# A gated linear recurrence and its MLP on one core: the score and state products laid into halves of the PE array's columns

## The chip, the cores and the metric

The kernel runs on one core of a Trainium2 chip, in one launch. The metric is the device time of that core in microseconds. The engines' short names are those of the profile: PE (TensorE, products), PEld (its weight loads, which may lie beside products), DVE (VectorE), ACT (ScalarE), POOL (GpSimd), and SP, whose queue issues the transfers.

## What is computed

A GateLoop recurrence for 4 sequences of 768 tokens, 8 heads of 48 elements each, followed by one MLP with the activation h * erf(softplus(h)):

```python
mag = np.sqrt(a_re * a_re + a_im * a_im)
scale = np.minimum(mag, 0.999) / (mag + 1e-06)
a_re_n, a_im_n = (a_re * scale, a_im * scale)
for t in range(S):
    new_re = ar * S_re - ai * S_im
    new_im = ar * S_im + ai * S_re
    S_re, S_im = (new_re + kv, new_im)          # kv: outer product of k and v of token t
    y[:, :, t] = np.einsum('bhd,bhde->bhe', q[:, :, t], S_re)
...
h = x @ w_in                                    # x: 3072 x 384, w_in: 384 x 2048
sp = np.maximum(h, 0.0) + np.log1p(np.exp(-np.abs(h)))
return (h * erf(sp)) @ w_out                    # w_out: 2048 x 384
```

All data is float32.

## The kernel before, in words

The path that runs is `quotient_path` (a second, slower path stands behind a test of the data at the end, and isn't taken here). It takes the recurrence in **chunks** of 128 tokens. Within a chunk the running product of the gates is a quotient of two prefix products, so that the tokens of a chunk meet in a masked product of queries and keys, as in linear attention, and chunks are joined by a state S. Two chunks make a **unit** of 256 tokens; there are 12 units, so 24 chunks, and six chunks make one sequence. The first chunk of a sequence has no state to read, the last one none to write.

Per unit, in the order of the work:

- `load_gates`, `load_qkv` (line 687): transfers on SP's queue. Values v go into one of two buffers `v0`, `v1`, by pairs of heads: 48 elements of the even head, a gap of 16 zeros, 48 of the odd head. `side` gives the part of one head. A transfer for each chunk and each of the two sides, four a unit.
- `g_mag` to `g_decay`: the gates' logarithms, angles and their prefix sums (the products `sum`, lines 818, 820 and 837), sines, and exponentials.
- `chunk(u, c)`: ten steps. `prep` (line 865) scales and turns k and q (tiles kt, qt: 128 tokens x 8 heads x 96). `cols` (line 876) turns four heads at a time so that the 96 elements lie on the partitions (products `tr`, line 880, then a copy: by ACT for k, by DVE for q). `state` (line 898) makes the chunk's sum of k v products, 96 x 48 for each head (`kv`, line 903), adds the old state and scales with w, the gates' product over the chunk (lines 912, 914). `scores` (line 887), once for each four heads: a product of 128 keys by 128 queries for each head (`sc`, line 891), then one DVE product with the upper triangle `triu` (line 894), which gives A. `xT` (line 917) makes the output of the chunk, already turned: the 384 output columns are cut in pieces of 32, each put into one quarter of the array's columns (`y`, line 940): v times A, and, but for the first chunk, the old state times q.
- `ff_in` (line 950): h = x w_in, 16 tiles of 128 columns in two slabs (`hps`, line 960), copied out by ACT. `softplus` (line 966): four activations over a slab of 2048 elements per partition. `erf_times_h` (line 978), in four parts of 512: Gelu on ACT into e (line 988), and four DVE operations (lines 989 to 992), the first of which writes the tile t. `ff_out` (line 996): the second product (`ops`, line 1006), then a copy and a transfer out.

Each engine works its instructions in order. The order is set in two steps: a list `plan` gives each step a due time in units (lines 1048 on), sorted before the program is recorded, and then a scheduler of the language may move an instruction past others on its engine where no data forbids it. Buffers are limited on purpose: z and yy of the softplus have one buffer, e two, A two (one for each four heads), kt one. PSUM has four pools of two buffers: `ps_a` for tr and sc, `ps_b` for sum, kv and y, `ps_h` for hps, `ps_o` for ops. Transfers wait on SP's queue in its order too.

In the profile a product in float32 appears as two passes, each a weight load (PEld) and a matmul (PE). In a form such as `128*32 128x128`, the first pair is rows and columns of the loaded weights, the second the streamed operand.

Of the kernel before, what the change touches and what calls it, by code (L numbers as in the profile page):

```python
# [10 lines left out]
FP = mybir.dt.float32  # L11
# [5 lines left out]
OP = mybir.AluOpType  # L17
PSUM = bass.MemoryType.PSUM

P = 128  # L20
# [27 lines left out]
def product_path(  # L48
# [280 lines left out]
    def attention(u, c, hg):  # L329
# [43 lines left out]
        def diag():  # L373
            lv = ps_lv.tile([P, HG, P], FP, tag="lv", name="dg")
            for j in range(HG):
                nc.tensor.matmul(out=lv[:, j, :], lhsT=st["K"][0:D2, j, :], rhs=st["q0"][0:D2, j, :],
                                 start=True, stop=True)
            A = att2.tile([P, HG, P], FP, tag="A", name="A")
            nc.vector.tensor_tensor(out=A, in0=lv, in1=ident.unsqueeze(1).to_broadcast([P, HG, P]), op=OP.mult)
            st["A"] = A  # L380

        def level(l):
            def f():
                m = 1 << l
                nb = P // (2 * m)
                Q, K, A, tot = st["Q"], st["K"], st["A"], st["tot"]
                Qv = Q.rearrange("p h (b w m) -> p h b w m", w=2, m=m)
# [5 lines left out]
                def halves(t, w):  # L393
                    return t.rearrange("p h (b w m) -> p (h b) w m", w=2, m=m)[:, :, w, :]
                nc.vector.copy_predicated(out=halves(A, 1), mask=pair[l], data=lv.rearrange("p h b m -> p (h b) m"))

# [160 lines left out]
def quotient_path(  # L557
# [19 lines left out]
    nc = tc.nc  # L577
    B, H, S, D = q.shape
    D2 = 2 * D
# [4 lines left out]
    C = 2  # L584
    NT = C * P
    PER = S // NT
    NU = B * PER
    HG = 4
# [6 lines left out]
    const = ctx.enter_context(tc.tile_pool(name="const", bufs=1))  # L595
# [4 lines left out]
    att1 = ctx.enter_context(tc.tile_pool(name="att1", bufs=1))  # L600
    att2 = ctx.enter_context(tc.tile_pool(name="att2", bufs=2))
# [3 lines left out]
    yp = ctx.enter_context(tc.tile_pool(name="yp", bufs=1))  # L605
    op = ctx.enter_context(tc.tile_pool(name="op", bufs=2))
# [7 lines left out]
    T = {}  # L614
# [1 line left out]

    ident = const.tile([P, P], FP, name="ident")
    make_identity(nc, ident)
    triu = const.tile([P, P], FP, name="triu")
    make_upper_triangular(nc, triu, val=1.0, diag=True)  # L620
    ones = const.tile([P, 1], FP, name="ones")
    nc.vector.memset(ones, 1.0)
# [13 lines left out]

    GAP, QUAD = 16, P // 4
    PAIR = 2 * D + GAP  # L640
    vbuf = [const.tile([P, C, H // 2, PAIR], FP, name=f"v{i}") for i in range(2)]
    sbuf = [const.tile([P, H // 2, PAIR], FP, name=f"S{i}") for i in range(2)]
    for t in vbuf:
        nc.vector.memset(t[:, :, :, D:D + GAP], 0.0)
# [3 lines left out]
    def side(t, e):  # L648

        return t[..., e * (D + GAP):e * (D + GAP) + D]  # L650
# [19 lines left out]
    def rows(a, u, c):  # L670
        b, s = divmod(u, PER)
        t0 = (s * C + c) * P
        return a[b, :, t0:t0 + P, :].rearrange("h t d -> t h d")
# [13 lines left out]
    def load_qkv(u):  # L687
        if 0 <= u < NU:
            load(ldq, "q", q, u)
            load(ldq, "k", k, u)  # L690
            t = T["v", u] = vbuf[u % 2]
            for c in range(C):
                for e in range(2):
                    src = rows(v, u, c).rearrange("t (h e) d -> e t h d", e=2)[e]
                    nc.sync.dma_start(out=side(t[:, c], e), in_=src)


    def narrow(i, dst, src, shape, home):
# [160 lines left out]
    def chunk(u, c):  # L859
# [3 lines left out]
        st = {}  # L863

        def prep(nm, e):
            def f():
                a = att1.tile([P, H, D], FP, tag="part", name=nm + "r", bufs=2)
                nc.vector.tensor_tensor(out=a, in0=T[nm, u][:, c], op=OP.mult,
                                        in1=T["pr", u][:, c, e, :].rearrange("p (h d) -> p h d", d=D))
                t = att1.tile([P, H, 2, D], FP, tag=nm + "t", name=nm + "t")  # L870
                cs = T["CS", u][:, c].rearrange("p u (h d) -> p h u d", d=D)
                nc.vector.tensor_tensor(out=t, in0=a.unsqueeze(2).to_broadcast([P, H, 2, D]), in1=cs, op=OP.mult)  # L872
                st[nm] = t
            return f
# [12 lines left out]
        def scores(g):  # L887
            def f():
                ps = ps_a.tile([P, HG, P], FP, tag="a", name="sc")
                for j in range(HG):  # L890
                    nc.tensor.matmul(out=ps[:, j, :], lhsT=st["k", g][0:D2, j, :], rhs=st["q", g][0:D2, j, :],  # L891
                                     start=True, stop=True)
                A = att2.tile([P, HG, P], FP, tag="A", name="A")
                nc.vector.tensor_tensor(out=A, in0=ps, in1=triu.unsqueeze(1).to_broadcast([P, HG, P]), op=OP.mult)
                st["A", g] = A
            return f

        def state():
            if last:
                return  # L900
            kv = ps_b.tile([P, H, D], FP, tag="b", name="kv")
            for j in range(H):
                nc.tensor.matmul(out=kv[0:D2, j, :], lhsT=st["k"][:, j].rearrange("p u d -> p (u d)"),  # L903
                                 rhs=side(T["v", u][:, c, j // 2], j % 2), start=True, stop=True)
            ns = sbuf[(u * C + c) % 2]
            w = T["w", u, c][0:D2].unsqueeze(2).to_broadcast([D2, H, D])
            if first:
                t = kv
            else:
                t = att1.tile([P, H, D], FP, tag="part", name="Skv", bufs=2)  # L910
                for e in range(2):
                    nc.vector.tensor_tensor(out=t[0:D2, e::2, :], in0=kv[0:D2, e::2, :], in1=side(T["S"][0:D2], e), op=OP.add)
            for e in range(2):
                nc.vector.tensor_tensor(out=side(ns[0:D2], e), in0=t[0:D2, e::2, :], in1=w[:, e::2, :], op=OP.mult)
            st["S"] = ns
# [62 lines left out]
    def erf_times_h(u, sl):  # L978

        n = SLAB // 4  # L980

        def part(i):
            def f():
                ss = slice(i * n, (i + 1) * n)
                h, z, y = (T[nm, u, sl][:, ss, :] for nm in ("h", "z", "yy"))
                t = yp.tile([P, n, NT], FP, tag="t", name="t")
                e = yp.tile([P, n, NT], FP, tag="e", name="e", bufs=2)
                act(out=e, in_=z, func=AF.Gelu, scale=RT2)
                nc.vector.tensor_tensor(out=t, in0=z, in1=y, op=OP.mult)  # L989
                nc.vector.scalar_tensor_tensor(out=y, in0=t, scalar=-2.0, in1=y, op0=OP.add, op1=OP.mult)  # L990
                nc.vector.tensor_tensor(out=e, in0=e, in1=y, op=OP.mult)  # L991
                nc.vector.scalar_tensor_tensor(out=h, in0=e, scalar=1.0 / RT2, in1=h, op0=OP.add, op1=OP.mult)  # L992
            return f
        return [part(i) for i in range(SLAB // n)]
# [50 lines left out]
    for cc in one:  # L1045
        g_sin(0, cc)

    plan = list(zip((0.50, 0.51, 0.52, 0.53, 0.55, 0.56, 0.60, 0.58, 0.59, 0.66), chunk(0, 0)))
    plan += list(zip((0.54, 0.57, 0.61, 0.62, 0.63, 0.64, 0.70, 0.68, 0.69, 0.74), chunk(0, 1)))
    plan += [(0.565, wt[0][2]), (0.645, wt[1][1]), (0.646, wt[1][2]), (0.71, wt[2][1]), (0.71, wt[2][2])]  # L1050
    plan += [(0.60, partial(load_qkv, 1))] + [(0.605, wt[j][0]) for j in (4, 5)]
# [9 lines left out]
    for j in range(6, len(wt)):  # L1061
        b = 1.45 + 1.1 * (j - 6) / (len(wt) - 6)
# [4 lines left out]
    for u in range(NU):  # L1067
        if u > 0:
            for c in range(C):
                b = begins[u][c] if u in begins else u + 0.5 * c  # L1070
# [10 lines left out]
        for sl in range(NSL):  # L1081
            b = u + 1.05 + 0.45 * sl
            plan += at(*(inputs[u][sl] if u in inputs else (b, b + 0.35)), ff_in(u, sl))
            b = u + 2.6 + 0.35 * sl
# [7 lines left out]
    n = len(seen)  # L1092
# [3 lines left out]
    ps = ps_b.tile([P, n], FP, tag="b", name="all")  # L1096
# [58 lines left out]
```

## Time and profile before

| | |
|---|---|
| three runs | 769.97, 774.02, 771.62 us; median 771.62 |
| the profiled execution | 771.92 us; the span of its instructions 770.1 us |
| mean granted clock of TensorE | 0.981 |
| instructions in the profile | 11542 |
| HBM read, written | 36.24 MB, 4.75 MB |
| transfers of v | 48 issues of 96 KB |

Where a page or a view says span, it counts from the first profiled instruction to the last; the 1.8 us between it and the execution's time lie around them. "Busy" is the time in which at least one instruction of a group is under way, so the mean length of a matmul, which holds its latency, times the count can be far over the busy time. A digit of a row by slices is the busy share of 19.25 us in tenths. In a group's line the last part is the time that the engine was idle just ahead of the group's instructions, and what ended most of it. An idle engine that isn't the bound costs nothing.

### The profile page before, as it was taken

Reading aid. Unit: us, or ns where it says so; the run is one execution under the profiler, and the core shown is the slowest. Engines: PE = TensorE matmul, PEld = TensorE weight load, DVE = VectorE, ACT = ScalarE, POOL = GpSimd, SP = SyncE. Lnnn points to the kernel's source line nnn. Section 1 sums busy time; section 2 is a strip of 40 time slices with the busy share of each in tenths; the row PEclk is TensorE's granted clock in tenths of the full one; section 3 lists DMA queues with packets and bytes.
Section 4 is the critical chain, followed back from the end, with each engine's and each line's share of the span. In section 5 each row is a group of like instructions: output and inputs, shape, how many; then the busy total and the mean of one; then the engine's idle time right before and its main releaser. Section 6 shows DMA issues by size and latency. Waiting matters only on the chain.

```text
span 770.1 us, 11542 instructions
## 1 busy us (share of the span) xinstructions
PE 720.1 (94%) x4524; PEld 542.0 (70%) x4524; DVE 535.7 (70%) x898; ACT 598.4 (78%) x815; POOL 1.1 (0%) x8
## 2 busy tenths in 40 slices
PE   1788869989999999999999999999999999999996
PEld 0566758866767777777777777777777777777553
DVE  5888978667887667567667668468567579765650
ACT  7889998698896993993993993993992888888810
POOL 0000000000000000000000000000000000000000
PEclk9998989999999999999999999999999999999998
DMA  8836456122212212212212212211112000000000
GB/s 218 219 109 163 103 114 179 29 41 43 41 43 52 42 32 53 43 31 52 42 32 52 42 31 47 48 31 38 16 32 42 1 21 1 1 22 0 21 20 26
DMA packets 148263, 41.84 MB, mean 54 GB/s; under 512 B 142292, under 2 KB 145384, under 8 KB 147432
## 3 DMA queue, kind: packets, MB, share of 16 engines
q1 hardware_dynamic: 148200, 41.02, 23.4%
q8 instruction: 37, 0.61, 0.3%
q14 instruction: 26, 0.21, 0.1%
HBM read 36.24 MB, written 4.75 MB: 53 GB/s over the span
## 4 chain that ended last, share of the span: by engine, by line
PE 62%; ACT 22%; DVE 9%; DMA 3%; issue 2%; SPq 1%; ACTq 0%; DVEq 0%
PE ops L1006 24%; PE hps L960 21%; ACT z L663 5%; ACT yy L663 4%; PE y L940 4%; PE sc L891 4%; PE tr L880 4%; ACT L662 3%; PE kv L903 3%; DVE t L989 2%; PE sum L818 2%; DVE yy L990 2%; PE sum L837 2%; DVE e L991 1%; ACT h L962 1%
## 5 line engine op out<-in xcount | busy, mean ns | idle before, releaser
L960 PE MATMUL hps<-xT,w_in_sb 128*128 128x256 f32 x1152 | 268.6, 383 | 4.4 <-ACT xT L944 2.6
L1006 PE MATMUL ops<-w_out_sb,h 128*128 128x384 f32 x768 | 267.2, 492 | 3.6 <-DVE h L992 2.8
L960 PEld LDWEIGHTS hps<-xT,w_in_sb 128*128 128x128 f32 x1152 | 217.0, 192 | 44.9 <-ACT xT L944 5.2
L1006 PEld LDWEIGHTS ops<-w_out_sb,h 128*128 128x128 f32 x768 | 141.8, 191 | 88.5 <-issue 5.3
L989 DVE TENSOR_TENSOR t<-z,yy 128x512 f32<-128x512 f32 x96 | 66.0, 688 | 57.5 <-ACT yy L663 56.9
L883 DVE COPY qT<-tr 96x512 f32<-96x512 f32 x48 | 32.8, 685 | 88.2 <-PE tr L880 88.1
L962 ACT COPY h<-hps 128x512 f32<-128x512 f32 x96 | 55.0, 575 | 50.0 <-PE hps L960 49.8
L662 ACT ACT_TABLE_LOAD x69 | 88.5, 1283 | 2.0 <-PEq L1139 0.8
L663 ACT ACTIVATE e<-z 128x512 f32<-128x512 f32 x96 | 57.4, 625 | 32.0 <-DVE h L992 31.8
L990 DVE SCALAR_TENSOR_TENSOR yy<-t,yy 128x512 f32<-128x512 f32 x96 | 66.0, 687 | 0.9
L991 DVE TENSOR_TENSOR e<-e,yy 128x512 f32<-128x512 f32 x96 | 64.8, 686 | 2.2 <-DVE yy L990 0.5
L992 DVE SCALAR_TENSOR_TENSOR h<-e,h 128x512 f32<-128x512 f32 x96 | 64.8, 686 | 0.2
L891 PE MATMUL sc<-qT,kT 96*128 96x128 f32 x384 | 50.4, 278 | 3.4 <-DVE qT L883 3.4
L891 PEld LDWEIGHTS sc<-qT,kT 96*128 96x128 f32 x384 | 47.7, 192 | 6.2 <-DVE qT L883 3.3
L940 PE MATMUL y<-A,v 128*32 128x128 f32 x768 | 47.6, 290 | 3.6 <-ACT pr L663 2.8
L663 ACT ACTIVATE z<-h 128x2048 f32<-128x2048 f32 x24 | 46.1, 1920 | 3.9 <-DVE t L989 3.8
L940 PEld LDWEIGHTS y<-A,v 128*32 128x32 f32 x768 | 34.7, 112 | 16.5 <-ACT pr L663 3.4
L663 ACT ACTIVATE yy<-z 128x2048 f32<-128x2048 f32 x24 | 45.9, 1913 | 0.4
L663 ACT ACTIVATE z<-z 128x2048 f32<-128x2048 f32 x24 | 45.9, 1912 | 0.4
L663 ACT ACTIVATE yy<-yy 128x2048 f32<-128x2048 f32 x24 | 45.9, 1912 | 0.2
L940 PE MATMUL y<-qT,S 96*32 96x128 f32 x640 | 41.0, 279 | 0.0
L880 PE MATMUL tr<-ident,kt 128*96 128x128 f32 x192 | 27.7, 280 | 8.0 <-DVE kt L872 7.6
(81 smaller groups left out, 792.2 us busy)
## 6 DMA issues: line engine op xcount, KB each, us to landing
raw<-in_moe_w_in_dram SPq DMA_DIRECT2D x6, 1024.0 KB, 7.2
raw<-in_moe_w_out_dram SPq DMA_DIRECT2D x8, 768.0 KB, 4.5
ar<-in_a_re_dram SPq DMA_DIRECT2D x24, 192.0 KB
ai<-in_a_im_dram SPq DMA_DIRECT2D x24, 192.0 KB, 3.5
q<-in_q_dram SPq DMA_DIRECT2D x24, 192.0 KB, 3.5
k<-in_k_dram SPq DMA_DIRECT2D x24, 192.0 KB, 3.2
v<-in_v_dram SPq DMA_DIRECT2D x48, 96.0 KB, 2.6
out_dram<-o SPq DMA_DIRECT2D x24, 192.0 KB, 1.9
```

The lines of the kernel that those rows point to most:

```text
L662: in_order(nc.scalar.preload_act_table_set(sets[0]))
L663: in_order(nc.scalar.activation(func=func, **kw))
L880: nc.tensor.transpose(out=ps[0:D2, j, :], in_=st[nm][:, g * HG + j].rearrange("p u d -> p (u d)"), identity=ident)
L891: nc.tensor.matmul(out=ps[:, j, :], lhsT=st["k", g][0:D2, j, :], rhs=st["q", g][0:D2, j, :], start=True, stop=True)
L940: nc.tensor.matmul(out=ps[b * QUAD:(b + 1) * QUAD, i, :], lhsT=lhsT, rhs=rhs, start=start, stop=stop)
L960: nc.tensor.matmul(out=ps[:, e, :], lhsT=w_in_sb[:, kd, f0:f0 + P], rhs=T["xT", u][:, kd, :], start=(kd == 0), stop=(kd == KD - 1))
L962: nc.scalar.copy(out=T["h", u, sl][:, i:i + 2, :], in_=ps)
L989: nc.vector.tensor_tensor(out=t, in0=z, in1=y, op=OP.mult)
L990: nc.vector.scalar_tensor_tensor(out=y, in0=t, scalar=-2.0, in1=y, op0=OP.add, op1=OP.mult)
L991: nc.vector.tensor_tensor(out=e, in0=e, in1=y, op=OP.mult)
L992: nc.vector.scalar_tensor_tensor(out=h, in0=e, scalar=1.0 / RT2, in1=h, op0=OP.add, op1=OP.mult)
L1006: nc.tensor.matmul(out=ps, lhsT=T["h", u, sl][:, e, jj * P:(jj + 1) * P], rhs=w_out_sb[:, i, :], start=(i == 0), stop=(i == KF - 1))
```

## The change

Five things are changed.

1. **Scores.** The score products of two heads are made as two pairs. The first pair takes keys 0 to 63 of each of the two heads against all 128 queries: the even head writes to PSUM partitions 0 to 63, the odd head to 64 to 127, so that they use different halves of the array's columns. The second pair takes keys 64 to 127 against queries 64 to 127 only, with the halves exchanged. The quarter of keys 64 to 127 and queries 0 to 63, which the mask makes zero, is left out; A is now two fixed buffers that are zeroed once. For odd heads the key halves stand exchanged on the partitions. The mask product is three DVE operations for four heads: one for the late 64 queries on all partitions, with a second mask `late` for the exchanged heads, and one each for the early queries of even and odd heads on 64 partitions.
2. **v.** As A of odd heads has its key halves exchanged, v of odd heads is loaded with its halves exchanged, in two transfers of 64 tokens, and once more in plain order into `odd0` or `odd1` for the state products. Eight transfers a unit, for four.
3. **State.** Each head's kv product is made as two of 64 columns, into PSUM partitions 0 to 63 and 64 to 127. The second takes columns 64 to 127 of a head's 96 in kt, so it runs 32 columns into its neighbour's; those results aren't read. kt is now a fixed buffer with 32 zeroed columns behind it.
4. **erf_times_h.** The tile t is gone: its product is written over z, which Gelu reads.
5. **The plan.** The state step of the very first chunk is due at 0.535 for 0.60, ahead of the preparation of the second chunk's k, which now writes the same fixed buffer.

```diff
-    triu = const.tile([P, P], FP, name="triu")
+    masks = const.tile([P, P + P // 2], FP, name="masks")
+    triu = masks[:, 0:P]
     make_upper_triangular(nc, triu, val=1.0, diag=True)
...
+    HALF = P // 2
+    abuf = [const.tile([P, 4, P], FP, name=f"A{i}") for i in range(2)]
+    for t in abuf:
+        nc.vector.memset(t, 0.0)
+    late = masks[:, HALF:].rearrange("p (e t) -> p e t", e=2)
+    nc.vector.tensor_copy(out=late[0:HALF, 1, :], in_=triu[0:HALF, 0:HALF])
+    nc.vector.memset(late[HALF:P, 1, :], 1.0)
+    kbuf = const.tile([P, H * 2 * D + P - 2 * D], FP, name="kt")
+    nc.vector.memset(kbuf[:, H * 2 * D:], 0.0)
...
+    vodd = [const.tile([P, C, H // 2, D], FP, name=f"odd{i}") for i in range(2)]
...
-                for e in range(2):
-                    src = rows(v, u, c).rearrange("t (h e) d -> e t h d", e=2)[e]
-                    nc.sync.dma_start(out=side(t[:, c], e), in_=src)
+                src = rows(v, u, c).rearrange("t (h e) d -> e t h d", e=2)
+                nc.sync.dma_start(out=side(t[:, c], 0), in_=src[0])
+                nc.sync.dma_start(out=vodd[u % 2][:, c], in_=src[1])
+                nc.sync.dma_start(out=side(t[HALF:P, c], 1), in_=src[1][0:HALF])
+                nc.sync.dma_start(out=side(t[0:HALF, c], 1), in_=src[1][HALF:P])
...
-                t = att1.tile([P, H, 2, D], FP, tag=nm + "t", name=nm + "t")
+                if nm == "k":
+                    t = kbuf[:, 0:H * 2 * D].rearrange("p (h u d) -> p h u d", h=H, u=2)
+                else:
+                    t = att1.tile([P, H, 2, D], FP, tag=nm + "t", name=nm + "t")
...
-                for j in range(HG):
-                    nc.tensor.matmul(out=ps[:, j, :], lhsT=st["k", g][0:D2, j, :], rhs=st["q", g][0:D2, j, :],
-                                     start=True, stop=True)
-                A = att2.tile([P, HG, P], FP, tag="A", name="A")
-                nc.vector.tensor_tensor(out=A, in0=ps, in1=triu.unsqueeze(1).to_broadcast([P, HG, P]), op=OP.mult)
-                st["A", g] = A
+                lo, hi = slice(0, HALF), slice(HALF, P)
+                for j in range(0, HG, 2):
+
+                    for keys, queries, out_ in ((lo, slice(0, P), (lo, hi)), (hi, hi, (hi, lo))):
+                        for e in range(2):
+                            nc.tensor.matmul(out=ps[out_[e], j + e, queries], lhsT=st["k", g][0:D2, j + e, keys],
+                                             rhs=st["q", g][0:D2, j + e, queries], start=True, stop=True)
+                A = st["A", g] = abuf[g]
+                pairs = lambda t: t.rearrange("p (h e) t -> p h e t", e=2)
+                nc.vector.tensor_tensor(out=pairs(A)[..., hi], in0=pairs(ps)[..., hi], op=OP.mult,
+                                        in1=late.unsqueeze(1).to_broadcast([P, HG // 2, 2, HALF]))
+                for e, r in enumerate((lo, hi)):
+                    nc.vector.tensor_tensor(out=A[r, e::2, lo], in0=ps[r, e::2, lo], op=OP.mult,
+                                            in1=triu[r, r].unsqueeze(1).to_broadcast([HALF, HG // 2, HALF]))
...
-                nc.tensor.matmul(out=kv[0:D2, j, :], lhsT=st["k"][:, j].rearrange("p u d -> p (u d)"),
-                                 rhs=side(T["v", u][:, c, j // 2], j % 2), start=True, stop=True)
+                val = vodd[u % 2][:, c, j // 2] if j % 2 else side(T["v", u][:, c, j // 2], 0)
+                for b in range(2):
+                    nc.tensor.matmul(out=kv[b * HALF:(b + 1) * HALF, j, :], rhs=val, start=True, stop=True,
+                                     lhsT=kbuf[:, j * D2 + b * HALF:j * D2 + (b + 1) * HALF])
...
-                t = yp.tile([P, n, NT], FP, tag="t", name="t")
                 e = yp.tile([P, n, NT], FP, tag="e", name="e", bufs=2)
                 act(out=e, in_=z, func=AF.Gelu, scale=RT2)
-                nc.vector.tensor_tensor(out=t, in0=z, in1=y, op=OP.mult)
-                nc.vector.scalar_tensor_tensor(out=y, in0=t, scalar=-2.0, in1=y, op0=OP.add, op1=OP.mult)
+                nc.vector.tensor_tensor(out=z, in0=z, in1=y, op=OP.mult)
+                nc.vector.scalar_tensor_tensor(out=y, in0=z, scalar=-2.0, in1=y, op0=OP.add, op1=OP.mult)
...
-    plan = list(zip((0.50, 0.51, 0.52, 0.53, 0.55, 0.56, 0.60, 0.58, 0.59, 0.66), chunk(0, 0)))
+    plan = list(zip((0.50, 0.51, 0.52, 0.53, 0.55, 0.56, 0.535, 0.58, 0.59, 0.66), chunk(0, 0)))
```

## The prediction, made before the changed kernel ran

> **What bounds the kernel now.** I read the page's first two parts, then the busy time by stretches of the span, then the groups of instructions, then a stretch of the timeline. The engines first; columns are busy time, share of the span, instructions, and below them the busy tenths of 40 slices of 19.25 us.
>
> ```profile
> PE 720.1 (94%) x4524; PEld 542.0 (70%) x4524; DVE 535.7 (70%) x898; ACT 598.4 (78%) x815; POOL 1.1 (0%) x8
> ...
> PE   1788869989999999999999999999999999999996
> ...
> DVE   5888978667887667567667668468567579765650
> ACT  7889998698896993993993993993992888888810
> ```
>
> TensorE is full from the seventh slice on; before that all engines are half full and none is. By stretches: 200 to 680 us has TensorE busy 118.3, 119.6, 119.6 and 120.0 of every 120 us, VectorE 83 to 84, ScalarE 94 to 98; 20 to 120 us has TensorE 80, VectorE 85, ScalarE 90 of 100. So some 20 of the 24 chunks lie where TensorE time is the kernel's time, and four lie in a start shared by VectorE, ScalarE and the transfers. What is to be changed there is small:
>
> ```profile
> L891 PE MATMUL sc<-qT,kT 96*128 96x128 f32 x384 | 50.4, 278 | 3.4 <-DVE qT L883 3.4
> L940 PE MATMUL y<-A,v 128*32 128x128 f32 x768 | 47.6, 290 | 3.6 <-ACT pr L663 2.8
> L903 PE MATMUL kv<-v,kt 128*96 128x48 f32 x320 | 31.9, 254 | 0.0
> ```
>
> Each product is two passes (192 score products give x384). The mean length of one holds pipeline latency; the price is the distance between starts, from the timeline (start, length):
>
> ```profile
> 400.98 1.48 PE L903 MATMUL kv<-v,kt 128*96 128x48 f32 x16
> 402.30 1.12 PE L891 MATMUL sc<-qT,kT 96*128 96x128 f32 x8
> 403.26 2.75 PE L1006 MATMUL ops<-w_out_sb,h 128*128 128x384 f32 x8
> ...
> 408.43 1.06 PE L891 MATMUL sc<-qT,kT 96*128 96x128 f32 x8
> 409.32 2.76 PE L960 MATMUL hps<-xT,w_in_sb 128*128 128x256 f32 x12
> 411.92 2.74 PE L1006 MATMUL ops<-w_out_sb,h 128*128 128x384 f32 x8
> 414.50 0.81 PE L818 MATMUL sum<-th,turns 128*128 128x384 f32 x2
> 415.24 0.43 PE L940 MATMUL y<-A,v 128*32 128x128 f32 x8
> ...
> 417.42 2.85 PE L1006 MATMUL ops<-w_out_sb,h 128*128 128x384 f32 x8
> 420.10 0.59 PE L960 MATMUL hps<-xT,w_in_sb 128*128 128x256 f32 x2
> ```
>
> Scores: 8 passes from 408.43 to 409.32, 0.112 us each. State: 16 passes in 1.32 us, 0.085 each apart from a short first. The 64 passes of y, in four column quarters, take 415.24 to 417.42, 0.034 each, though each streams as many columns as a score pass: quarters do run beside each other. But they have a price at the edges. Two passes of 384 columns cost 2.58/8 = 0.323 each, so sum should end at 415.15; y starts at 415.24 (0.09 late). The ops behind y take 2.68 to the next group, those ahead of it 2.58 (0.10 more: the first weights were not loaded beside earlier work). Between the last y pass (its four-row piece starts at 417.06, 0.42 long, passes 0.27: last start 417.21) and ops lie 0.21 instead of 0.11 (0.10).
>
> [...]
>
> **The change part by part.**
>
> Scores: a pair of heads was 4 passes at 0.112 = 0.448 us. Now each half of the columns gets two passes of 128 queries (0.112) and two of 64 [...], both halves at once: 0.340. A chunk of 4 pairs: 1.79 to 1.36.
>
> State: a chunk's 16 passes at 0.085, plus 0.07 [...] (kv and sc: 400.98 to 403.26 is 2.28 = 1.32 + 0.90 + 0.06), is 1.39. Now 16 passes in each half at 0.058: 0.93.
>
> Mode visits: every run of such products between products of the whole array pays 0.09 in, 0.05 for a first 64-column load that nothing hides (half of the 0.10 of 128), 0.10 out, 0.10 for the load after: 0.34 us. y's visits are there already. Whether the visit with halves costs what that with quarters does no row shows: from 0.10 [...] to 0.4; I take 0.34. The order of the changed kernel's instructions has, in a usual first chunk, kv alone and the scores of all heads together: 1.39+1.79 = 3.18 becomes 0.93+0.34+1.36+0.34 = 2.97. In a second chunk kv goes straight into half the scores: 2.28+0.90 = 3.18 becomes 0.93+0.68+0.34 and 0.68+0.34 = 2.97. A sequence's last chunk has no state: 1.79 becomes 1.70. So a chunk as meant gains 0.1 to 0.2 us. But in that order other products split more runs (kv into 3 and 13, 4 and 12, 7 and 9, 11 and 5, scores around a sum): 43 visits stand in TensorE's stretch. There 16 chunks with a state and 20 with scores give up 16*0.46 + 20*0.43 = 16.0 us of products, and the visits bring 43*0.34 = 14.6 back. **TensorE: -1.4 us.**
>
> VectorE: the mask product of 512 elements (0.684) becomes one of 256 and two of 128 on half the partitions. From the A row and the state row (96x192, 0.346), 1.06 ns an element: 0.41+2*0.28 = 0.97, +0.29, 48 times: 13.8 us more on an engine with 36 of 120 us free. In the busy stretch it hides unless A comes late for y. The added memsets and small copies of the constants are some 1.3 us (2 of 512 elements at about 1 ns, from the memsets of v) and fall into the 4.11 us in which VectorE's first product waits for a transfer. With z written in place, the first product of a slab waits for Gelu: table load 1.28 plus 0.63 after the last Exp, where t started at once (400.69, with yy and whole behind it). Queued behind it on VectorE is the rest of the slab, and ScalarE's third Gelu waits for that. The order groups these as two z, two yy, two e, two h, so about 2 us a slab later; a slab's h is not read for some 10 us (the last: written 740.6, its first product needed near 752), so ScalarE's and VectorE's slack hides it. If not, 2 us of 24 slabs show.
>
> Transfers: v needs four more issues a unit (8 for 4). v's four took 2.46 us on SP's queue at 11.5, 0.62 each: up to 2.5 us a unit, and 192 KB more, 0.9 us at the first slices' 218 GB/s. In the full stretch SP waits more than it works (178 us on o alone) and DMA is at a tenth or two: nothing. In the start, with DMA at eight tenths, three units' loads stand ahead of weights, gates and w on SP. From 0 to 7.5 us; I take 2.5, with the four start chunks' 2.3 us of VectorE among it. State moved ahead (0.60 to 0.535): kv stood among the q transposes already; it issues products alone, no transfer. Nothing.
>
> Late masks: A of 412.59 to 413.87 stood 1.4 us ahead of y. It comes 0.6 us later by its own length and more by the grouped erf work; the new order puts 3 more ops products (6 passes, 1.9 us) between second scores and y. I take 0.5 us in all.
>
> Sum, against the profiled execution's own 771.9 (span 770.1), 0.3 above the median of 771.6: 771.9 - 1.4 + 2.5 + 0.5 = 773.5, say **773**.
>
> **Rivals.** *Visits are cheap.* [...] a visit costs 0.14: 43 times 0.2 = 8.6 less, 765. [...] Against: both edges of y show the price whole. *VectorE's mask is late* (slower): each unit has one place where both erf blocks lie between the two score masks. If the second half of a mask is done behind a block of eight erf products (8 at 0.6 = 4.8 us), y waits and with it TensorE, for its work is in order. It decides from the point where A comes later than the 5.2 to 7.1 us of other products between scores and y; an overrun of 0.8 us in ten units is 8 us: 781. For it: VectorE has no gap from 400.7 to 415.2. Against: the order has the added filler. *The halves don't overlap*, the change doesn't do what it says: kv 1.86+0.34, scores 2.72+0.34, 2.1 us a chunk more, 20 times: 815. y's 0.034 speaks against it.
>
> **How the numbers follow.** Near even 0.46 (its own range 768 to 778), cheap visits 0.20, late masks or a start that pays in full 0.29, no overlap 0.05. The last and a little of each end are left out: 763 to 783. A measurement here tells 0.5%, 3.9 us, from no change. Faster: the cheap case and a little of the even one, 0.22. Slower: the late and no-overlap cases and a sixth of the even one, 0.42. Between, 0.36.
>
> **What would show it.** Timeline: 64-column kv passes in both halves, 16 pairs in some 0.93 us; scores of a chunk 1.36; the product ahead of and behind each run 0.1 late. Groups: three mask rows near 0.41, 0.28. TensorE in 200 to 680 us still full. Wrong if y's idle before it grows (late masks), if the edges cost under 0.2 in all, if the halves' passes start in turn, or if TensorE gets idle after the start.

## The result, and the profile after

The changed kernel takes 778.75 us (median of 4 runs, 777.83 to 779.84) where the kernel before takes 771.77 (769.97 to 774.02): 1.0089 times as long, 95% interval 1.006 to 1.0119, so 7.0 us slower. The forecast was 773, 1.4 us more than before. The time lies inside the stated range (763 to 783), but 5.6 of the 7.0 us were not in the likeliest case.

The page of the changed kernel, engines and slices of 19.4 us:

```profile
span 777.1 us, 13064 instructions
...
PE 721.2 (93%) x5228; PEld 526.3 (68%) x5228; DVE 550.5 (71%) x999; ACT 598.8 (77%) x815; POOL 1.1 (0%) x8
...
PE   2688869989999999999999999999999999999994
...
DVE  5799987838978688488488478388578568655660
ACT  7779988599698886994993993994983887778750
```

TensorE is busy about as long as before (721.2 for 720.1) with 704 passes more, and the span grew by 7.0. So most of the added time isn't TensorE's busy time. The changed rows, all of one view of groups by form:

```profile
L1018 DVE TENSOR_TENSOR z<-z,yy 128x512 f32<-128x512 f32 x96 | 62.1, 686 | 38.1 <-ACT e L678 37.7
...
L915 PE MATMUL sc<-qT,kT 96*64 96x128 f32 x384 | 37.7, 287 | 1.8 <-DVE qT L903 1.8
...
L915 PE MATMUL sc<-qT,kT 96*64 96x64 f32 x384 | 28.7, 225 | 0.0
L922 DVE TENSOR_TENSOR A<-sc,masks 64x128 f32<-64x128 f32 x96 | 27.3, 284 | 1.1
L933 PE MATMUL kv<-v,kt 128*64 128x48 f32 x320 | 22.9, 238 | 0.1
...
L919 DVE TENSOR_TENSOR A<-sc,masks 128x256 f32<-128x256 f32 x48 | 20.3, 423 | 15.5 <-PE sc L915 14.0
```

The masks have the lengths that were forecast (0.42 and 0.28 us), 47.6 us busy for 32.4. The first row is the error function's first product, now written over z: VectorE stood idle 37.7 us for Gelu (e) ahead of it. In the kernel before it stood idle longer there, but for the softplus (yy), which stands ahead of Gelu:

```profile
L989 DVE TENSOR_TENSOR t<-z,yy 128x512 f32<-128x512 f32 x96 | 66.0, 688 | 57.5 <-ACT yy L663 56.9
```

So what changed is not the idle time but what VectorE waits for; what that made late is asked below.

What it costs to go from products of the whole array to products in its halves, and back, is read from the timeline of TensorE (start, length):

```profile
404.76 0.81 PE L835 MATMUL sum<-th,turns 128*128 128x384 f32 x2
405.50 0.32 PE L933 MATMUL kv<-v,kt 128*64 128x48 f32 x4
...
406.35 0.29 PE L933 MATMUL kv<-odd,kt 128*64 128x48 f32 x4
406.47 0.85 PE L915 MATMUL sc<-qT,kT 96*64 96x128 f32 x16
407.25 2.85 PE L1035 MATMUL ops<-w_out_sb,h 128*128 128x384 f32 x8
409.93 2.75 PE L990 MATMUL hps<-xT,w_in_sb 128*128 128x256 f32 x12
412.62 0.89 PE L915 MATMUL sc<-qT,kT 96*64 96x128 f32 x16
413.44 2.86 PE L990 MATMUL hps<-xT,w_in_sb 128*128 128x256 f32 x12
416.13 4.68 PE L1035 MATMUL ops<-w_out_sb,h 128*128 128x384 f32 x14
```

Two sum passes at 0.323 end at 405.41, kv starts at 405.50: 0.09 for going in. All 32 kv passes take 405.50 to 406.47, 0.97. The ops passes behind the visit take 2.68 to the next group, where 8 at 0.323 make 2.58: 0.10 more. The first of them starts together with its own weight load (both at 407.25), where the first hps pass, at 409.93, starts 0.32 behind its load (409.61); so the 0.10 is put down to that first weight load.

**Where 7.0 us went.** I give every pass the price that its product had in the kernel before (a chunk's state and scores as wholes), and compare the times at which two kernels have done the same sum. Against the kernel before, the changed kernel is 3.5 us late at 155 us, 3.0 at 264 us, 4.7 at the last product; and the end, from the start of the last ops pass on, is 10.4 us for 8.1 (the text of e1 below counts it from the product of the data test behind that pass, 10.0 for 7.7). So: start +3.5, the stretch to 264 -0.5, the full stretch behind it +1.7, the end +2.3; together 7.0, the difference of the spans.

The start of one execution is a draw: the traces of the kernel before and of e2, with the same order of all products, lay 5.3 us apart at 155 us (TensorE's granted clock is 0.90 in one and 0.84 in the other between 20 and 120 us) and then stayed within 0.05 us of each other for 600 us. So starts are compared by the times of all runs, and the full stretch, here all that lies behind 264 us, by the traces, where 0.1 us counts.

The clock of a whole execution goes with its time as well: among the 45 executions of the kernel before that ran beside e5 to e8, 0.01 of mean clock goes with 3.1 us (an estimate, by a straight line). The executions of e5 had 0.976 in the mean, those of e7 0.984, the kernel before 0.980. So some 1.4 us of what e5 loses below, and 1.3 of what e7 gains, may be the clock's; whether those changes bring it about or it is chance, no run shows. (e6, which has z in place too, loses 3.6 us at 0.980.)

### The profile page after: what moved, and what is told of

Its sections match the earlier page's. It is cut to its first block, busy times and chain, and to the rows that moved or that the text cites. A ratio compares the mean times of both kernels' runs of the same rounds, so it can differ in the third digit from the quotient of the medians.

```text
span 777.1 us, 13064 instructions
## 1 busy us (share of the span) xinstructions
PE 721.2 (93%) x5228; PEld 526.3 (68%) x5228; DVE 550.5 (71%) x999; ACT 598.8 (77%) x815; POOL 1.1 (0%) x8
## 4 chain that ended last, share of the span: by engine, by line
PE 60%; ACT 22%; DVE 12%; issue 2%; DMA 2%; SPq 0%; ACTq 0%; DVEq 0%
PE hps L990 22%; PE ops L1035 21%; PE tr L900 4%; PE y L970 3%; PE sc L915 3%; ACT L677 3%; ACT yy L678 3%; ACT z L678 3%; DVE z L1018 2%; DVE yy L1019 2%; PE sum L835 2%; PE kv L933 2%; DVE e L1020 2%; ACT pr L678 1%; ACT CS L678 1%
## 5 line engine op out<-in xcount | busy, mean ns | idle before, releaser
L990 PE MATMUL hps<-xT,w_in_sb 128*128 128x256 f32 x1152 | 273.4, 387 | 8.6 <-ACT h L992 5.7
L1018 DVE TENSOR_TENSOR z<-z,yy 128x512 f32<-128x512 f32 x96 | 62.1, 686 | 38.1 <-ACT e L678 37.7
L1021 DVE SCALAR_TENSOR_TENSOR h<-e,h 128x512 f32<-128x512 f32 x96 | 62.2, 684 | 0.1
L1019 DVE SCALAR_TENSOR_TENSOR yy<-z,yy 128x512 f32<-128x512 f32 x96 | 62.1, 684 | 0.0
L1020 DVE TENSOR_TENSOR e<-e,yy 128x512 f32<-128x512 f32 x96 | 62.1, 684 | 0.0
L970 PE MATMUL y<-A,v 128*32 128x128 f32 x768 | 47.6, 286 | 5.0 <-ACT pr L678 3.0
L915 PEld LDWEIGHTS sc<-qT,kT 96*64 96x64 f32 x768 | 36.7, 141 | 10.8 <-issue 3.9
L915 PE MATMUL sc<-qT,kT 96*64 96x128 f32 (+1 forms) x768 | 41.7, 256 | 1.8 <-DVE qT L903 1.8
```

The source lines that it names most:

```text
L915: nc.tensor.matmul(out=ps[out_[e], j + e, queries], lhsT=st["k", g][0:D2, j + e, keys], rhs=st["q", g][0:D2, j + e, queries], start=True, ...
L970: nc.tensor.matmul(out=ps[b * QUAD:(b + 1) * QUAD, i, :], lhsT=lhsT, rhs=rhs, start=start, stop=stop)
L990: nc.tensor.matmul(out=ps[:, e, :], lhsT=w_in_sb[:, kd, f0:f0 + P], rhs=T["xT", u][:, kd, :], start=(kd == 0), stop=(kd == KD - 1))
L1018: nc.vector.tensor_tensor(out=z, in0=z, in1=y, op=OP.mult)
L1019: nc.vector.scalar_tensor_tensor(out=y, in0=z, scalar=-2.0, in1=y, op0=OP.add, op1=OP.mult)
```

## The experiments

Twelve kernels. The columns in the middle are us against the kernel before in one execution of each: at 155 us, then gained or lost up to 264, up to the last product, and behind it. The ratio is of times, with its 95% interval, against the kernel before as it ran beside each. The changed kernel's own interval is 2.3 us to either side: by the times alone, another kernel's difference from it of under 3 us can't be told from none (an estimate from the intervals).

| kernel | at 155 | to 264 | to last product | end | median | ratio |
|---|---|---|---|---|---|---|
| changed | +3.5 | -0.5 | +1.7 | +2.3 | 778.75 | 1.0089 (1.0060 to 1.0119) |
| e1 changed, no second path | +0.4 | +0.7 | +1.7 | -3.8 | 773.16 | 1.0013 (1.0000 to 1.0025) |
| e2 before, no second path | +5.3 | 0 | 0 | -3.8 | 768.23 | 0.9952 (0.9938 to 0.9967) |
| e3 changed, odd from GpSimd | +2.6 | -0.5 | +2.6 | +1.8 | 778.91 | 1.0092 (1.0070 to 1.0114) |
| e4 changed, states whole | +7.0 | -0.5 | +4.1 | +0.4 | 782.03 | 1.0122 (1.0099 to 1.0144) |
| e5 before, z in place | +1.4 | -0.1 | +1.9 | +0.1 | 776.14 | 1.0052 (1.0030 to 1.0073) |
| e6 e5 and eight transfers | +1.1 | 0 | +1.9 | 0 | 775.20 | 1.0046 (1.0026 to 1.0066) |
| e7 before, three masks | -3.2 | -0.6 | +0.5 | +0.2 | 769.03 | 0.9962 (0.9948 to 0.9976) |
| e8 before, states in halves | +0.3 | -0.4 | +0.9 | +0.4 | 772.12 | 1.0009 (0.9989 to 1.0029) |
| e9 changed, own tile for t | +2.6 | -3.2 | +3.3 | +1.8 | 776.87 | 1.0066 (1.0040 to 1.0091) |
| e10 changed, scores whole | +3.1 | +0.8 | +2.1 | +1.5 | 778.31 | 1.0081 (1.0058 to 1.0105) |
| e11 changed, due together | +1.6 | -1.1 | +13.8 | 0 | 786.26 | 1.0170 (1.0146 to 1.0195) |
| e12 e9 and e11 | +2.4 | -3.2 | +2.0 | 0 | 772.36 | 0.9995 (0.9983 to 1.0007) |

### The end: e1 and e2

```diff
         with tc.If(fine < 1):
-            product_path(tc, q, k, v, a_re, a_im, w_in, w_out, out)
+            nc.vector.memset(ok, 0)
```

> Changed kernel with the second, slower path behind the test of the data left out (it isn't taken with these data; only a write of one flag stands there). The order of all products is that of the changed kernel. Theory: the 2.3 us by which the end after the last product grew (from 7.7 to 10.0 us) belong to TensorE's instruction stream around the branch over that path, since the last event of the profile is TensorE's, 2.2 us behind all other engines. Then the end shrinks to 7.8 us or less and the time is about 776.5 us. Rival (the end grew for another reason, a transfer or the test itself): the end stays at 10.0 us and the time at 778.8.

> Kernel before with the second path left out in the same way. Theory: all engines of the kernel before ended together, so nothing of its end hung on that path: 771.8 us, end after the last product 7.7 us. Rival (the path costs in both kernels, by its length): the end shrinks by 1 to 3 us here as well, and the time with it.

Both shrank, the changed kernel by 5.6 us (778.75 to 773.16) where 2.3 was forecast, the kernel before by 3.5 (771.74 to 768.23). The theory of e2 falls; its rival holds, with somewhat more than its 1 to 3 us: the path that isn't taken costs in both. The end is 4.3 us without it, in either kernel. The lines of the branch show where (PEldq is TensorE's own sequencer; the figures are lengths in ns, then the starts of the first and the last); changed kernel first:

```profile
L1152 DVEq COMPARE_BRANCH  x1: 72/72/72, 769.3 to 769.3; - x1
L1152 PEldq COMPARE_BRANCH  x1: 4165/4165/4165, 769.3 to 769.3; - x1
```

```profile
L1179 DVEq EVENT_SEMAPHORE  x2: 21/21/21, 774.3 to 774.9; - x2
L1179 PEldq EVENT_SEMAPHORE  x2: 51/51/51, 774.3 to 777.0; - x2
```

The kernel before:

```profile
L1123 PEldq COMPARE_BRANCH  x1: 4358/4358/4358, 764.6 to 764.6; - x1
```

```profile
L1150 PEldq EVENT_SEMAPHORE  x2: 51/51/51, 769.5 to 770.1; - x2
```

The changed kernel without the path:

```profile
L1152 PEldq COMPARE_BRANCH  x1: 223/223/223, 767.4 to 767.4; - x1
```

TensorE's branch over the path takes 4.2 to 4.4 us, 0.22 when nothing lies behind it; VectorE's takes 0.07. That is the part common to both. The changed kernel pays 2.1 to 2.3 us more: its very last instruction on TensorE comes at 777.0 when VectorE's last comes at 774.9; in the kernel before the last instructions of both come at 770.1. That the extra goes with the path is seen in e1, where it is gone. That it follows from the number of instructions is not seen: e11 has the changed kernel's count of products and none of the extra (end 8.05 us), e9 and e10 have 1.5 to 1.8 of it, e4 0.4. Each kernel has one trace, so it isn't shown either whether the extra belongs to a kernel or to an execution. What decides stays open.

### The start: e3, e6, e7

In the trace of the changed kernel the transfer of plain odd values for a buffer that is still read held SP's queue until 101 us, and the raw weights stood behind it:

```profile
100.98 0.37 SPq L710 DMA_DIRECT2D odd<-in_v_dram  x1
101.44 0.46 SPq L724 DMA_DIRECT2D raw<-in_moe_w_out_dram  x1
```

```diff
-                nc.sync.dma_start(out=vodd[u % 2][:, c], in_=src[1])
+                nc.gpsimd.dma_start(out=vodd[u % 2][:, c], in_=src[1])
```

> Changed kernel, with the one transfer of plain odd values (for the state products) issued from GpSimd's queue instead of SP's. Theory: the start lost 2.8 us because that transfer, for the unit whose buffer is still read by state products, held SP's queue, and the raw weights of the second product behind it; on another queue it holds nobody: the transfer of the raw weights is issued some 3 us earlier than 101.4 us, products behind 150 us run 2.5 to 3 us earlier, the time is about 776 us. Rival (the added bytes or issues, or the longer mask work of VectorE, made the start late): the same work is still there, and the time stays within 0.5 us of 778.8.

The weights' transfer is issued earlier:

```profile
99.88 0.38 SPq L724 DMA_DIRECT2D raw<-in_moe_w_out_dram  x1
```

That is 1.6 us earlier, not the 3 that were forecast: in e3 the transfer of the raw weights waits itself, 7.5 us by SP's timeline (92.38 to 99.88). In the kernel before such transfers wait for ACT's work on the buffer that they fill (five times, 22.6 us in all). The time is the same (778.91). The odd values' wait, plain to see in the queue, stood in front of another nearly as long, and taking it away gained nothing.

e6 asks after all transfers together, on the kernel before:

```diff
-                    nc.sync.dma_start(out=side(t[:, c], e), in_=src)
+                nc.sync.dma_start(out=side(t[:, c], 0), in_=src[0])
+                nc.sync.dma_start(out=vodd[u % 2][:, c], in_=src[1])
+                nc.sync.dma_start(out=side(t[HALF:P, c], 1), in_=src[1][HALF:P])
+                nc.sync.dma_start(out=side(t[0:HALF, c], 1), in_=src[1][0:HALF])
...
```

> The same with a second part of the change: v is loaded by eight transfers a unit instead of four (odd heads once in plain order and once in two halves, not exchanged here since A isn't), and the state products read odd heads from the plain copy. No product, mask or mode is changed. What the start lost, some 3 us in the changed kernel, is in question. Theory (transfers, the prediction's 2.5 us): 2 to 3 us slower than with z in place alone. Rival (the start pays for VectorE's masks or TensorE's visits, since moving one of the three added issues to another queue gained nothing): within 0.7 us of it.

775.20 against 776.14 for z in place alone, and by the ratios 0.5 us less, give or take 2.3: no loss is seen, and the rival holds. The times of e6 fall in two groups, though, 11 under 775.4 and 8 from 777.5 to 780.8; one of the 7 of e5 lies as high. What makes the second group isn't known. And the masks, on the kernel before:

```diff
-                nc.vector.tensor_tensor(out=A, in0=ps, in1=triu..., op=OP.mult)
+                nc.vector.tensor_tensor(out=A[:, :, hi], in0=ps[:, :, hi], op=OP.mult, in1=triu[:, hi]...)
+                for e in range(2):
+                    nc.vector.tensor_tensor(out=A[lo, e::2, lo], in0=ps[lo, e::2, lo], op=OP.mult, in1=triu[lo, lo]...)
```

> Kernel before with whole products, but its mask made as the change makes it: three VectorE operations of 256, 128 and 128 elements into two fixed buffers A that are zeroed once, in plain order for all heads (the quarter of late keys and early queries is computed and not used). VectorE gets 0.29 us more for each of 48 masks, 13.8 in all, and 1 us of memsets. Theory (the four chunks of the start pay in VectorE's own time, 8 masks of 0.29, and the memsets, 3.3 us; the full stretch hides the rest): 773.5 to 775. Rival (hidden throughout): 771.7, within 0.5. Second rival (late masks: y waits in the full stretch): 777 or more, with y's idle grown.

769.03, 0.9962 times before (0.9948 to 0.9976): with three masks that kernel is **faster** by 3.3 us, which none of the theories had. Behind 155 us its trace gains nothing (-0.6, +0.5 and +0.2), so the gain lies in the start. Between 20 and 120 us VectorE is busy 90.4 of 100 us, for 85.3 in the kernel before, only part of which is longer masks (8 masks of 0.2 to 0.3 us): it waits less. Its waits for the turned q, between 15 and 125 us, fall from 8.3 to 2.7, while those for kv grow (in all, times, longest; the kernel before, then e7):

```profile
DVE qT L883 <- PE tr L880: 8.3, 3, 5.9
DVE Skv L912 <- PE kv L903: 1.4, 2, 0.8
```

```profile
DVE Skv L921 <- PE kv L912: 3.0, 2, 2.5
DVE qT L888 <- PE tr L885: 2.7, 4, 1.0
```

The order on the engines differs there too (all eight second-chunk scores now stand together ahead of y). Whether the fixed A, the shorter masks, that order or a better clock brings it, this run doesn't separate.

### z in place: e5 and e9

```diff
-                t = yp.tile([P, n, NT], FP, tag="t", name="t")
...
-                nc.vector.tensor_tensor(out=t, in0=z, in1=y, op=OP.mult)
+                nc.vector.tensor_tensor(out=z, in0=z, in1=y, op=OP.mult)
...
```

> Kernel before with one part of the change alone: the tile t is gone, and the first product of the error function's steps is written over z, which Gelu reads. TensorE's products and their number are those of before. In the changed kernel TensorE is idle 1.9 us more between 276 and 680 us, with waits for ACT's copies of h. Theory: that comes from z in place, since VectorE's product waits for Gelu and ACT's next Gelu for VectorE: 1.5 to 2.5 us slower than before, 773.2 to 774.2. Rival (the prediction's step: ScalarE's and VectorE's slack hides it, and the idle time comes from the masks or the visits): 771.7, within 0.5.

776.14, +3.8 us, twice what the theory said and far from the rival. In the full stretch it loses 1.9 us, all of it waits; the other 1.9 lie in the start, where part may be the clock's. What TensorE waits for between 276 and 680 us (in all, times, longest), in e5:

```profile
PE tr L880 <- DVE kt L872: 1.9, 6, 0.4
PE tr L880 <- ACT kT L883: 0.3, 1, 0.3
```

In the changed kernel:

```profile
PE tr L900 <- DVE kt L892: 1.3, 2, 0.7
PE hps L990 <- ACT xT L974: 0.9, 3, 0.3
PE tr L900 <- ACT kT L903: 0.4, 1, 0.4
```

(The kernel before has 0.4 us in all, for xT.) So it isn't h that is late, but **kt**, the next chunk's scaled k, which VectorE makes. Why is seen on VectorE's timeline of the changed kernel:

```profile
328.75 0.29 DVE L922 TENSOR_TENSOR A<-sc,masks 64x128 f32<-64x128 f32 x1
329.70 1.29 DVE L1018 TENSOR_TENSOR z<-z,yy 128x512 f32<-128x512 f32 x2 [0.66 <-ACT e L678]
330.91 1.29 DVE L1019 SCALAR_TENSOR_TENSOR yy<-z,yy 128x512 f32<-128x512 f32 x2
...
335.11 1.28 DVE L1018 TENSOR_TENSOR z<-z,yy 128x512 f32<-128x512 f32 x2
...
338.72 1.29 DVE L1021 SCALAR_TENSOR_TENSOR h<-e,h 128x512 f32<-128x512 f32 x2
339.93 0.55 DVE L1039 TENSOR_SCALAR o<-ops 128x384 f32<-128x384 f32 x1
340.39 0.95 DVE L892 TENSOR_TENSOR kt<-kr,CS 128x768 f32<-128x768 f32 x1
```

The kernel before, the same place of the work:

```profile
321.56 0.68 DVE L990 SCALAR_TENSOR_TENSOR yy<-t,yy 128x512 f32<-128x512 f32 x1
322.16 0.68 DVE L894 TENSOR_TENSOR A<-sc,triu 128x512 f32<-128x512 f32 x1
...
331.78 0.69 DVE L992 SCALAR_TENSOR_TENSOR h<-e,h 128x512 f32<-128x512 f32 x1
332.38 0.96 DVE L872 TENSOR_TENSOR kt<-kr,CS 128x768 f32<-128x768 f32 x1
```

With t, some of the error function's products run earlier, between the masks. With z in place none can start before Gelu has read z, so all 16 operations of the slab stand behind the masks in two blocks of 4.8 us, and kt behind both: 340.39 for 332.38, 8 us later, where TensorE is only 4 us later. CS, which it reads, is done at 338.5 for 332.2 (ACT's third Gelu waits 1.81 us for VectorE's h), and for the 1.9 us from there on kt stands behind VectorE's other work. The next tr waits for it. e5, whose edit holds nothing else, has the same two blocks and this kt, 5.4 us later than in the kernel before where TensorE is 1.3 us later:

```profile
337.76 0.94 DVE L872 TENSOR_TENSOR kt<-kr,CS 128x768 f32<-128x768 f32 x1
```

e9 gives the changed kernel a tile for t again:

```diff
+                t = tmp.tile([P, n, NT], FP, tag="m", name="t")
...
-                nc.vector.tensor_tensor(out=z, in0=z, in1=y, op=OP.mult)
+                nc.vector.tensor_tensor(out=t, in0=z, in1=y, op=OP.mult)
...
```

> Changed kernel, with the product of the error function's steps written into a tile of its own again (it shares the place of a temporary tile of the gates' steps, as there is no other room). Theory (z in place cost 3.8 us in the kernel before, and the changed kernel pays it too): about 3.8 us faster than the changed kernel, 775.0, with TensorE's idle time between 276 and 680 us back at 1 us. Rival (in the changed kernel the idle time comes from masks or visits): 778.8, within 0.7.

The waits for kt are gone (0.6 us for kT are left; TensorE's idle time from 276 to 680 us is 0.8, for 2.7), but the time falls by 1.9 us only, which by the intervals could as well be nothing or the whole forecast. The trace says more: behind 264 us the kernel with t is even 1.6 us slower. The blocks of products show why: in this order y comes in 23 pieces behind 264 us, for 16, and they take 37.3 us for 32.3. A y of 64 passes takes 2.28 from the product ahead to the one behind; cut in 26 and 38 it takes 1.13 + 1.54, 0.39 more, and 0.10 more in the product behind. So the theory is right about the wait and not about the sum, since the order of the instructions moved as well.

### The products: e4, e8, e10

e4 makes the changed kernel's states whole again; e8 puts them into halves in the kernel before; e10 makes the scores whole again. The edit of e4, which e8 makes the other way:

```diff
-                for b in range(2):
-                    nc.tensor.matmul(out=kv[b * HALF:(b + 1) * HALF, j, :], rhs=val, ...
-                                     lhsT=kbuf[:, j * D2 + b * HALF:j * D2 + (b + 1) * HALF])
+                nc.tensor.matmul(out=kv[0:D2, j, :], rhs=val, ..., lhsT=kbuf[:, j * D2:(j + 1) * D2])
```

> Changed kernel, with the state's products whole again (96 columns of a head at once, as before the change), scores still in halves. Visits of the halves' mode fall from 51 to 36, since 15 of them held state products alone. By the prediction's prices: products grow by 0.46 us in each of 20 chunks, 9.2 us (7.4 in TensorE's full stretch), and 15 visits of 0.34, 5.1 us, go: about +2.3 us, 781 us. Rival A (a visit costs about 0.6 or more, the halves of the state aren't worth it): 777 us or less. Rival B (a visit costs 0.15 or less): 784 us or more.

> Kernel before with the state's products alone in halves of the columns (kt a fixed buffer, the first state at 0.535); scores, masks, v and z as before. Twenty chunks give up 0.46 us each, 9.2 us, and 22 visits at 0.34 bring 7.5 back: 1.7 us faster by the prediction's prices, 770.0. By the step of the changed kernel against its form with whole states (3.3 us for the state in halves, with 15 visits more): at 20*0.46 - 15*p = 3.3 a visit costs p = 0.39, and here 9.2 - 22*0.39 = 0.6 us faster, 771.1. Rival (a visit costs 0.2): 4.8 us faster, 767.

> Changed kernel, with the score products alone whole again (128 keys by 128 queries of each head; odd heads not exchanged, so v's odd halves are loaded in plain order); masks in three operations, eight transfers of v, states in halves, z in place stay. Visits fall from 51 to 25. By the prediction's prices: products grow by 0.43 in 24 chunks, 10.3 us, and 26 visits of 0.34 go, 8.8: 1.5 us slower than the changed kernel, 780. Rival (the parts add up: before 772.3, z in place +3.8, eight transfers -0.9, three masks -3.3, states in halves -0.2 to +0.7, in all 771.7 to 772.6, so that the score halves are what the change loses by): about 772.

e4 is at 782.03, 3.3 us slower than the changed kernel where 2.3 was forecast. The full stretch has 2.4 of it; the start is slower too and the end 1.9 us shorter, so that the total agrees partly by luck. e8 is at 1.0009 (0.9989 to 1.0029): no difference, which rules out the 1.7 us and more of the forecast and the rival, and not the 0.6; its blocks of kv and sc give up 1.5 us behind 264 us, but TensorE waits for ACT's copy kT, 2.5 us where the kernel before shows none. e10 is at 778.31, within 0.5 us of the changed kernel: its prices said 1.5 slower, the rival 6 faster. The rival falls; 1.5 can't be told from nothing by the times, and in the full stretch e10 is 0.4 us slower. So each half of the change is worth between nothing and some 3 us as far as these runs tell, and neither is what the change loses by.

The prices themselves come out of the blocks of the traces, counted from the end of the product ahead to the start of the one behind. Medians in the changed kernel, in us: 32 kv passes alone 1.162; 16 sc passes alone 0.912; both in one visit 1.845, so a visit costs 1.162 + 0.912 - 1.845 = 0.23, and the 0.10 of the first weight load behind it: **0.33 us**. Two runs of 16 sc, 1.824, against 32 in one, 1.582, give 0.24 and 0.10.

### Fewer visits: e11 and e12

```diff
-STEPS = (0.0, 0.03, 0.06, 0.09, 0.12, 0.15, 0.2, 0.25, 0.28, 0.4)
+STEPS = (0.0, 0.03, 0.06, 0.09, 0.12, 0.15, 0.35, 0.351, 0.352, 0.4)
```

> Changed kernel, with the due times of a chunk's state and scores set together (0.35, 0.351 and 0.352 of a unit instead of 0.2, 0.25 and 0.28; the output stays at 0.4), so that they mostly follow each other in one visit of the halves' mode: 33 visits instead of 51, the same products. Theory (a visit costs 0.34): 18 visits less, 6.1 us faster than the changed kernel, 772.6. Rival A (visits cost half): 775.7. Rival B (A comes late for y, since scores stand nearer to it): no gain, with y's idle grown.

> Both edits: the tile of its own for that product, and state and scores due together; 37 visits. Theory: 3.8 us by the tile and 13 to 14 visits of 0.34, 4.6 us, less than the changed kernel: 770.4, a little faster than the kernel before (772). Rival (the gains don't add, as both fill the same idle time of TensorE): 772.6 or more.

e11 is **7.5 us slower** than the changed kernel, and neither for the visits nor for A. Its waits of TensorE, 276 to 680 us:

```profile
PE ops L1035 <- DVE h L1021: 9.9, 6, 3.1
PE ops L1035 <- DVE o L1039: 3.2, 6, 1.2
...
PE y L970 <- DVE A L922: 0.2, 1, 0.2
```

The same order with a tile for t, e12:

```profile
PE y L970 <- DVE A L922: 1.9, 3, 1.1
PE ops L1036 <- DVE h L1022: 0.8, 1, 0.8
```

With z in place the second product of the MLP waits 9.9 us for h, which the prediction held to be 10 us early; with t, 0.8. Bringing the visits together moved the work, and the error function in place had no room left. e12 is 4.5 us faster than e9, and 13 visits of 0.34 would make 4.4; that agreement is luck, as 1.8 of it lie in the end, the full stretch gains 1.3, and A now comes late for y (1.9 us). It ends level with the kernel before: 0.9995 (0.9983 to 1.0007). The forecast of 770.4 lies just outside that interval; the time is nearer the rival's 772.6 or more, which it just misses. Of all that ran with the second path, e7 alone beats both.

## Why the prediction was right and where it was wrong

That 778.75 lies in the range is in good part luck. It lies just above the even case's own 768 to 778, among the slower cases, and the causes that these had, late masks, a start that pays for all its transfers and halves that don't overlap, were not found. Of the terms of the sum the products came out, z in place was put at nothing and cost, the start came late by another cause, and the end was missing.

- **Products: right.** A chunk's state was put at 0.93 and its scores at 1.36; the blocks give 1.162 - 0.23 = 0.93 and 1.582 - 0.24 = 1.34. (The 1.39 that it set against the state is its 1.32 plus 0.07; 16 passes at 0.085 plus 0.07, as it says, would be 1.43.) The 0.058 us that it took for a pass of 64 columns was its author's estimate; kv's groups of 4 passes, two in each half, start 0.117 us apart (405.65 to 406.35 in six steps), 0.058 a pass in each half. A visit was put at 0.34 and is 0.33, of it 0.09 going in and 0.10 in the product behind it; how the rest divides isn't shown. Behind 264 us the blocks of kv and sc fell from 39.96 to 35.75 us, and 27 first products behind them pay 0.10 each: -4.2 + 2.7 = -1.5 us. The -1.4 of the forecast is for more chunks (20) and more visits (43); at its prices the 11 states, 14 chunks' scores and 27 visits behind 264 us give 5.1 + 6.0 - 9.2, so -1.9. The prices are right within 0.4 us there; that -1.5 is so close to -1.4 is chance. The rivals of cheap visits (0.14) and of halves that don't overlap (1.86 us for the 32 kv passes that take 0.97) are out.
- **Masks: right in effect.** +15.2 us busy for the 13.8 forecast. That was an estimate from two rows of the kernel before, 684 ns for the mask of 512 elements and 346 for the state's 192; it gave 0.41 and 0.28 us for the new masks, and 423 and 284 ns are measured. TensorE's waits in the full stretch show none for A: the rival of late masks did not come, nor did the 0.5 us. The one y that was cut in two costs 0.4 instead.
- **z in place: wrong.** The step said that a slab's h is not read for some 10 us, "so ScalarE's and VectorE's slack hides it". It looked at who reads h, and not at what else stands behind the error function on VectorE. kt does, and TensorE's turning of k waits for it: 1.9 us in the full stretch of e5, where its whole time grows by 3.8 (2.3 to 5.6). The other branch of the step, "2 us of 24 slabs show", would have been far too much.
- **The start: wrong causes, nearly the right sum.** 2.5 us were put on it, for the added issues and with 2.3 us of VectorE's masks among them. But the eight transfers show no cost (e6), one fewer on SP's queue gains nothing (e3), and three masks by themselves (e7) gain 3.3 us. The start lost about 3 us all the same: 7.0 less what the traces show behind it. z in place may hold 1.4 to 1.9 of it (e5's trace at 155 us, and e5's time less its full stretch), if that isn't the clock; the rest doesn't come from any part tried alone. The parts don't add there. The order on VectorE differs between these kernels from 20 us on. What of it decides stays open.
- **The end: missing.** No step looked behind the last product. The changed kernel's trace has 2.3 us more there, though no line of it was changed.

In figures, for the full stretch: -1.5 for products, +0.4 for the cut y, and +2.8 of waits and other delay among products of the whole array (5.5 by the starts of the passes, less the 2.7 of first weight loads), which makes its +1.7. Of the 2.8 I put 1.9 down to z in place, since it alone cost that in e5, and TensorE's idle time fell by that with t in e9; the other 0.9 isn't traced. With about 3 for the start, near the forecast but not by its causes, and 2.3 for the end, which no step had, that is the 7.0.

## What to carry to other kernels

When a step gets a new wait, list what stands *behind* it on its engine (here kt on VectorE, 8 us later) and who reads that, not only who reads its own result. Where halves or quarters of the array are visited between whole products, price the visit (here 0.33 us for halves, 0.49 for cutting a quarter's run in two) against what a run of products saves (0.46 us for a chunk's state), and remember that the runs which share a visit are set by the order, which any other edit moves. Try the parts of a change alone: here one small part that touches no product cost, alone, about half as much as the whole change, and another one alone went with a gain.

## What the runs showed that was not expected

- The branch over the second path, which is never run, took 4.2 to 4.4 us on TensorE's sequencer and 0.05 to 0.07 us on the others; leaving the path out takes 3.5 us (kernel before) and 5.6 us (changed) off the median.
- In both pairs of traces with one order of products (before and e2, changed and e1) the two repeat each other within 0.05 us from 200 us to the last product; what they differ by, 5.3 and 1.9 us, is made ahead of that.
